# A fused chunk-attention and Mish feed-forward kernel: attention steps of the next tokens spread over two units, weight sums loaded one unit ahead, operands of x built in small steps

## The chip, the cores and the metric

The kernel runs on one core of one Trainium2 chip. The metric is device time in microseconds, median over the runs. Times are in us unless marked otherwise.

## The reference

Attention inside chunks of 64 tokens, then a feed-forward block with Mish (h tanh(softplus(h))), for 8 batches, 8 heads, 576 positions and head size 64, that is 4608 tokens of width 512 and a hidden width of 2048, all in float32.

```python
scores = scale * np.matmul(q_c, k_c.transpose(0, 1, 2, 4, 3))
scores = scores - np.max(scores, axis=-1, keepdims=True)
attn = np.exp(scores)
attn = attn / (np.sum(attn, axis=-1, keepdims=True) + 1e-09)
out = np.matmul(attn, v_c)
...
h = x @ w_in
sp = np.where(h > 20.0, h, np.log1p(np.exp(np.minimum(h, 20.0))))
g = h * np.tanh(sp)
return (g @ w_out).astype(np.float32)
```

The two weight matrices arrive as 64-bit floats and are turned into float32 by integer operations on the chip.

## The kernel before

**Precision.** The matmuls of the feed-forward block take operands in a reduced form of float32. Each operand is split into a high part (a cast on ACT or DVE) and a low part (a subtraction on DVE), and each product is three matmuls: low x high, high x low, high x high.

**Tokens.** A "pair" is two tiles of 128 tokens. The 18 pairs are worked off in five groups: two pairs first (512 tokens), then four quads of four pairs (1024 tokens each).

**First group.** `prologue` (line 469) does attention of the first two pairs. Then 16 `slot`s (line 543) run, one for each 128 columns of the hidden width (f = 0 to 15): `up` is the product with w_in, `mish` the activation on ACT, `g_split` makes gh and gl, and `down` queues 12 matmuls (4 token tiles x 3) of the product with w_out in the list `fill`, which `filled(n)` issues later. Beside this the slots load and convert the weights (`w_load` to `w_keep`; 32 blocks) and do attention of quad 1's four pairs, by the table `first_plan` (line 538).

**Quads.** The product with w_in uses a seven-product scheme (Strassen's in Winograd's form), with halves of the tokens and of the contraction: A11, A12, A22 are blocks of weights, S1 to S4 sums of blocks; B11, B21, B22 and T1 to T4 are the same of x. `s_load` (line 174) loads a converted block pair (cs) into the tile bld, and `s_build` (line 182) forms the four sums on DVE (line 195), a cast on ACT (196), the low part on DVE (197), and stores both to DRAM as sa. This happens once for each of the eight units, u = 0 to 7: two builds in the last two slots and six in quad 1's units, each load directly ahead of its build. `load_op` (line 630) loads one operand (w_A from ra or w_S from sa) six products ahead. `x_sums` (376) and `x_split` (367) make T1 to T4 and the parts of all seven operands of x, in two halves, out of `raw`, the result of attention.

**Unit** (line 696): seven products of six matmuls each go into the PSUM tiles x, y and v (two buffers). Between them stand 3 to 5 matmuls of `fill`, 24 in a unit. ACT and DVE turn the sums into four results: two (a1, a2) are split and queued for `down` at once, two (b1, b2) are kept in zb for the second half of the tokens. `phase_two` (line 750) does `down` for these, 16 f's of 12 matmuls. The results accumulate in PSUM banks o_(m, 0) and o_(m, 1); `store` (line 452) copies four tiles of them to the buffers ob (three) and then to DRAM. New banks can only begin where the old ones have been copied.

**Attention beside a quad.** The steps for a pair are a_scores (PE), a_max and a_sub (DVE), a_exp (ACT), a_inverse and a_norm (DVE), a_transpose (PE), a_copy (ACT), a_values (PE), a_raw (ACT). In the kernel before they follow the table `plan` (line 660) by ticks: three ticks in a unit and one for each step of phase_two. A pair's scores, exp, norm, transposes and values lie in consecutive ticks; the fourth pair's transposes and values fall into phase_two.

**Order.** The program runs under a manual schedule: each engine works its instructions in the order in which the code issues them, and waits at each for its operands and buffers. The loads, and the stores to DRAM, are on SP's queue, which is in order as well.

Of the kernel before, what the change touches and what calls it, by code (L numbers as in the profile page):

```python
# [14 lines left out]
ALU = mybir.AluOpType  # L15
# [8 lines left out]
def kernel(  # L24
# [149 lines left out]
    def s_load(u):  # L174
        if "t" not in bld:
            bld["t"] = zb_p.tile([P, 16 * 256], F32, name="bld", tag="z")
        t = bld["t"]
        nc.sync.dma_start(
            out=t[:, 0 : 2 * DM], in_=w_c[u].rearrange("p h c -> p (h c)")
        )  # L180

    def s_build(u):
# [6 lines left out]
        for out_, x, y, op in (  # L189
            (s1, a21, a22, ALU.add),  # L190
            (s2, s1, a11, ALU.subtract),
            (s3, a11, a21, ALU.subtract),
            (s4, a12, s2, ALU.subtract),
        ):
            nc.vector.tensor_tensor(out=out_, in0=x, in1=y, op=op)
        nc.scalar.copy(out=o[:, :, 0].bitcast(F32R), in_=s)
# [179 lines left out]
    def x_sums(m, half):  # L376
        for out_, x, y in (
            ("T1", "B12", "B11"),
            ("T3", "B22", "B12"),
            ("T2", "B22", "T1"),  # L380
            ("T4", "B21", "T2"),
        ):
            nc.vector.tensor_tensor(
                out=raw_half(m, half, out_),
                in0=raw_half(m, half, x),
                in1=raw_half(m, half, y),
                op=ALU.subtract,
            )
# [149 lines left out]
    first_plan = {}  # L538
    for i, k0 in enumerate((1, 4, 7, 10)):
        for n in range(-2, 4):  # L540
            first_plan.setdefault(k0 + n, {})[n] = first_pair(1) + i

    def slot(s):
        a = first_plan.get(s, {})
# [4 lines left out]
        if 3 in a:  # L549
            a_values(a[3])  # L550
        if s < NF - 1:
            filled()
        if 2 in a:
            a_norm(a[2])
            a_transpose(a[2])
        if 0 in a:
            a_scores(a[0])

# [3 lines left out]
        down(0, s, it[s])  # L562
# [3 lines left out]
        if 1 in a:  # L566
            a_max(a[1])
            a_sub(a[1])

        w("load", n + 5)  # L570
        w("keep", n)
        if 3 in a:
            a_raw(a[3])
        if 2 in a:
            a_copy(a[2])
# [8 lines left out]
        if 1 in a:  # L584
            a_exp(a[1])
            a_inverse(a[1])
        if -2 in a and a[-2] > 2:
            load_qk(a[-2], pool=(xo_p, "x"))
        if s == NF - 1:
            load_qk(first_pair(2))  # L590
        if 0 in a:
            load_v(a[0])
        if s == 9:
            x_split(1, 0, "B11", "B21")
        if s == 10:
# [12 lines left out]
        if s == 15:
            x_sums(1, 1)
            x_split(1, 1, "T2", "T1", "T3", "T4")  # L610
            s_load(1)
            s_build(1)
# [45 lines left out]
    TICKS = 3 * NU + NU  # L658
    plan = {}
    for i, k0 in enumerate((1, 8, 15, 22)):  # L660
        for n in range(0, 5):
            plan.setdefault(k0 + n, {})[n] = i
        plan.setdefault(max(0, k0 - 3), {})[-3] = i

    def pair_at(m, tick, n):
        i = plan.get(tick, {}).get(n)
        return None if i is None or m == QUADS else first_pair(m + 1) + i

    def on_tensor(m, tick):
        for n, step in ((3, a_transpose), (4, a_values), (0, a_scores)):  # L670
            j = pair_at(m, tick, n)
            if j is not None:
                step(j)

    def beside(m, tick):
        for n, steps_ in (
            (-3, () if tick == 0 else (load_qk,)),
            (0, (load_v, a_max, a_sub)),
            (1, (a_exp, a_inverse)),
            (2, (a_norm,)),  # L680
            (3, (a_copy,)),
            (4, (a_raw,)),
        ):
            j = pair_at(m, tick, n)
            for step in steps_ if j is not None else ():
                step(j)

    zb = {}
    BUILD = {0: 2, 2: 3, 4: 4, 6: 5, 8: 6, 10: 7}

    def build(m, tick):
        if m == 1 and tick in BUILD:
            s_load(BUILD[tick])
            s_build(BUILD[tick])

    def unit(m, u):
        tick = 3 * u
# [9 lines left out]
        on_tensor(m, tick)  # L707
# [5 lines left out]
        build(m, tick)  # L713
        beside(m, tick)

        product(m, u, 2, x, False)
        filled(3)
        nc.scalar.copy(out=b1, in_=x)  # L718
        on_tensor(m, tick + 1)
        y = ps_h.tile([P, TOK], F32, name=f"v_{m}_{u}", tag="h")  # L720
        product(m, u, 3, y, True)
        filled(5)
        g_split(a1, a1["z"], f"{m}_{2 * u}")
        build(m, tick + 1)
        beside(m, tick + 1)

        product(m, u, 4, x, False)
        filled(3)
        nc.scalar.copy(out=b2, in_=x)  # L729
        on_tensor(m, tick + 2)  # L730
        filled(2)
        product(m, u, 5, x, False)
        add(y, b2)
        a2["z"] = z_tile(f"z_{m}_{2 * u + 1}")
        mish(a2["z"], x)
        product(m, u, 6, y, False)
# [13 lines left out]
    def phase_two(m):  # L750
        after = m < QUADS
        p = first_pair(m)
        for i in range(NU):
# [3 lines left out]
            if i == 0:  # L757
                store(f"{m}a", (p, p + 2))
# [74 lines left out]
```

## Time and profile before

| | |
|---|---|
| median of 3 runs | 980.69 (980.15 to 981.61) |
| the profiled execution | 983.48, its span 981.6 |
| PE busy | 854.0 (87%), 5724 matmuls |
| DVE busy | 439.5 (45%) |
| ACT busy | 381.3 (39%) |
| DMA | 137.25 MB, 140 GB/s on average |
| mean granted TensorE clock | 0.942 |

The profile shows one execution. PE is the matmul engine, PEld its weight loads, DVE the vector engine, ACT the scalar engine, SPq the queue of DMA issues. A row names the line of the kernel, the engine, the operation, the tiles written and read (buffer numbers left out), and the shapes. Its times are busy time in total and the mean of one instruction in ns, then the idle time before it and what ended that. In rows by time the first number is the start and the second the duration; a matmul's duration includes its way through the array, so the distance between starts says what it costs. The granted clock is a share of full speed.

### The profile page before, as it was taken

The numbers are of one execution on the slowest core, as the hardware profiler recorded it, in microseconds if no ns is written. First come the engines' busy times: TensorE is split into PE (matmuls) and PEld (weight loads), VectorE is DVE, ScalarE is ACT, GpSimd is POOL, SyncE is SP. The second block draws the span as 40 slices with busy tenths as digits, with TensorE's granted clock in tenths as the row PEclk, the third lists the DMA queues.
The fourth block names the chain that finished last, engine by engine and source line by source line (L and its number), as shares of the span: only waits on it lengthen the run. The fifth ranks groups of instructions, "written<-read, shape, count | busy, mean of one in ns | idle before, by whom it ended". The sixth has DMA issues, their size and how long they took to land.

```text
span 981.6 us, 14157 instructions
## 1 busy us (share of the span) xinstructions
PE 854.0 (87%) x5724; PEld 690.9 (70%) x5724; DVE 439.5 (45%) x678; ACT 381.3 (39%) x584; POOL 0.7 (0%) x6
## 2 busy tenths in 40 slices
PE   4988855468599979989999799899997999999897
PEld 3866744356487858768778587687785877888685
DVE  6788983432524354433343444433424543223221
ACT  4878851322334233343342433433433433222221
POOL 0000000000000000000000000000000000000000
PEclk9899996778899989999999899999998999999999
DMA  6989816556554530256455301554453016444201
GB/s 247 334 291 302 284 67 228 179 175 201 171 184 131 170 85 21 68 127 185 149 140 165 93 22 44 151 182 146 135 152 95 1 43 161 119 130 120 52 1 43
DMA packets 68577, 137.25 MB, mean 140 GB/s; under 512 B 7072, under 2 KB 13216, under 8 KB 67488
## 3 DMA queue, kind: packets, MB, share of 16 engines
q1 hardware_dynamic: 68224, 135.82, 45.5%
q8 instruction: 46, 0.75, 0.3%
q10 hardware_dynamic: 288, 0.52, 0.1%
q14 instruction: 19, 0.16, 0.1%
HBM read 108.00 MB, written 28.31 MB: 139 GB/s over the span
## 4 chain that ended last, share of the span: by engine, by line
PE 65%; DVE 13%; ACT 7%; DMA 7%; issue 3%; SPq 1%; ACTq 0%; DVEq 0%
PE x L644 16%; PE v L644 8%; PE y L644 4%; DMA bld<-cs 3%; PE o_(4, 1)_0_7181 L435 2%; PE o_(4, 0)_0_6431 L435 2%; PE o_(4, 1)_2_7188 L435 2%; PE o_(1, 1)_0_2904 L435 2%; PE o_(3, 1)_0_6000 L435 2%; PE o_(2, 1)_0_4452 L435 2%; PE o_(4, 0)_2_6448 L435 2%; PE o_(1, 1)_2_2911 L435 2%; PE o_(2, 1)_2_4459 L435 2%; PE o_(3, 1)_2_6007 L435 2%; PE o_(3, 0)_0_4931 L435 2%
## 5 line engine op out<-in xcount | busy, mean ns | idle before, releaser
L644 PE MATMUL x<-x_T,w_S 128*128 128x512 f32 x384 | 102.7, 404 | 16.0 <-ACT zb L718 8.0
L656 DVE TENSOR_TENSOR zb<-v,zb 128x512 f32<-128x512 f32 x64 | 44.2, 690 | 126.4 <-PE v L644 94.8
L644 PEld LDWEIGHTS x<-x_T,w_S 128*128 128x128 f32 x384 | 74.3, 195 | 33.5 <-ACT zb L718 9.3
L422 DVE CAST gh<-z 128x512 fp32r<-128x512 f32 x72 | 30.5, 423 | 114.9 <-PE o_(4, 0)_2_6448 L435 28.4
L644 PE MATMUL x<-x_B,w_A 128*128 128x512 f32 x192 | 50.8, 401 | 12.9 <-DMA w_A<-ra 12.9
L294 PE MATMUL pt<-ident,p 128*128 128x128 f32 x144 | 24.3, 321 | 42.7 <-DVE p L285 35.6
L729 ACT COPY zb<-x 128x512 f32<-128x512 f32 x32 | 18.8, 587 | 108.6 <-PE x L644 108.6
L424 DVE TENSOR_TENSOR gl<-z,gh 128x512 fp32r<-128x512 f32 x80 | 55.4, 693 | 9.8 <-ACT gh L420 7.4
L294 PEld LDWEIGHTS pt<-ident,p 128*128 128x128 f32 x144 | 19.3, 165 | 49.2 <-issue 38.8
L415 ACT ACTIVATE z<-z 128x512 f32<-128x512 f32 x32 | 20.2, 632 | 86.6 <-DVE z L656 86.6
L644 PE MATMUL y<-x_B,w_A 128*128 128x512 f32 x192 | 53.6, 418 | 0.0
L656 DVE TENSOR_TENSOR z<-y,z 128x512 f32<-128x512 f32 x32 | 22.1, 690 | 69.7 <-PE y L644 69.7
L644 PEld LDWEIGHTS x<-x_B,w_A 128*128 128x128 f32 x192 | 36.4, 192 | 22.7 <-ACT x_T L371 13.3
L402 PE MATMUL h<-x_first,wi 128*128 128x512 f32 (+1 forms) x204 | 51.4, 407 | 0.7 <-ACT x_first L334 0.7
L644 PE MATMUL x<-x_T,w_A 128*128 128x512 f32 x192 | 50.8, 401 | 0.0
L644 PE MATMUL v<-x_T,w_S 128*128 128x512 f32 x192 | 50.5, 398 | 0.1
L415 ACT ACTIVATE zb<-zb 128x512 f32<-128x512 f32 x64 | 39.6, 627 | 25.1 <-DVE zb L656 25.1
L644 PE MATMUL v<-x_B,w_S 128*128 128x512 f32 x192 | 49.0, 391 | 0.0
L402 PEld LDWEIGHTS h<-x_first,wi 128*128 128x128 f32 x204 | 39.4, 208 | 8.6 <-ACT x_first L334 0.9
L415 ACT ACTIVATE z<-x 128x512 f32<-128x512 f32 x32 | 19.1, 597 | 67.5 <-PE x L644 67.4
L644 PEld LDWEIGHTS y<-x_B,w_A 128*128 128x128 f32 x192 | 38.4, 204 | 8.8
L644 PEld LDWEIGHTS x<-x_T,w_A 128*128 128x128 f32 x192 | 37.6, 196 | 8.4
(197 smaller groups left out, 1794.7 us busy)
## 6 DMA issues: line engine op xcount, KB each, us to landing
w_S<-sa SPq DMA_DIRECT2D x128, 256.0 KB, 3.2
w_A<-ra SPq DMA_DIRECT2D x96, 256.0 KB, 2.8
wst<-in_w_in SPq DMA_DIRECT2D x16, 512.0 KB, 5.8
wst<-in_w_out SPq DMA_DIRECT2D x16, 512.0 KB, 5.7
q<-in_q SPq DMA_DIRECT2D x16, 512.0 KB, 4.0
k<-in_k SPq DMA_DIRECT2D x16, 512.0 KB, 5.6
v<-in_v SPq DMA_DIRECT2D x16, 512.0 KB, 4.5
sa<-bld SPq DMA_DIRECT2D x8, 1024.0 KB, 4.9
```

Source lines behind the costliest of these rows:

```text
L294: nc.tensor.transpose(out=d["pt", ts.start][:, t - ts.start, g], in_=d["p"][:, t, g].rearrange("p c k -> p (c k)"), identity=ident,)
L402: nc.tensor.matmul(h[:, cols], lhsT=wi[i][:, w_, kt], rhs=x[:, x_, kt, cols], start=(n == 0), stop=(n == 3 * NK - 1),)
L415: nc.scalar.activation(out=out_, in_=in_, func=AF.Mish)
L422: nc.vector.tensor_copy(out=d["gh"], in_=z)
L424: nc.vector.tensor_tensor(out=d["gl"], in0=z, in1=d["gh"].bitcast(F32), op=ALU.subtract)
L435: nc.tensor.matmul(acc[t], lhsT=g[:, t * P : (t + 1) * P], rhs=w_[:, f], start=(f == 0 and n == 0), stop=(f == NF - 1 and n == 2),)
L644: nc.tensor.matmul(o, lhsT=t[:, w_, kt], rhs=x[x_][:, kt], start=(start and i == 0), stop=(i == 5), skip_group_check=not start,)
L656: nc.vector.tensor_tensor(out=z, in0=o, in1=z, op=ALU.add)
L729: nc.scalar.copy(out=b2, in_=x)
```

## The change

The computation and the number of instructions of each kind on PE and DVE stay the same. What changes is where they stand.

1. *Builds.* `s_build(u)` itself issues the load of the next block pair after its four sums. `s_load(0)` goes to slot 13, `s_build(0)` to slot 14 ahead of the x steps, `s_build(1)` to slot 15 behind them. Builds 2 to 7 are spread over units 0 to 3 of quad 1, at two places in a unit. Two of the first six operand loads go ahead of `s_load(0)`.
2. *Attention in the slots* follows two tables by half slots, `on_pe` and `beside_pe`, and takes seven half slots for a pair. `filled()` and `down` move behind the first half's work on ACT and DVE.
3. *Attention in the units.* Each pair takes two units: scores after product 0 of the even unit, max and sub after product 1, exp after product 2, inverse after product 3, norm after product 4, transposes and copy at its end; values and raw in the odd unit, and the loads of the next q and k behind them. The last pair's raw waits for phase_two.
4. *Unit.* `filled` is dealt out as 3, 5, 4, 4, 5 and the rest. Copy, add and mish of b2 follow product 4. In unit 0 the whole fill is issued after product 4 and the store of the previous group follows there, instead of after the unit.
5. *phase_two* goes by single f's: 12 matmuls, the split of one f, then two of the 23 small x steps. The store comes at f = 1.

```diff
@@ s_load, s_build
     def s_load(u):
+        if u >= NU:
+            return
...
             nc.vector.tensor_tensor(out=out_, in0=x, in1=y, op=op)
+        s_load(u + 1)
         nc.scalar.copy(out=o[:, :, 0].bitcast(F32R), in_=s)
@@ x
+    X_STEPS = [
+        ("B11",),
+        ("B21",),
+        ("B22",),
+        ("T1", "B12", "B11"),
+        ("T3", "B22", "B12"),
+        ("T2", "B22", "T1"),
+        ("T4", "B21", "T2"),
+        ("T2",),
+        ("T3",),
+        ("T1",),
+        ("T4",),
+    ]
+
+    def x_step(m, half, n):
+        step = X_STEPS[n]
+        if len(step) == 1:
+            x_split(m, half, *step)
+        else:
+            x_sum(m, half, *step)
@@ slots
-    for i, k0 in enumerate((1, 4, 7, 10)):
...
+    for i, h0 in enumerate((1, 8, 15, 22)):
+        j = first_pair(1) + i
+        for n, step in ((0, a_scores), (5, a_transpose), (6, a_values)):
+            on_pe.setdefault(h0 + n, []).append((step, j))
+        for n, steps_ in (
+            (0, (load_v,)),
+            (1, (a_max, a_sub)),
+            (2, (a_exp,)),
+            (3, (a_inverse,)),
+            (4, (a_norm,)),
+            (5, (a_copy,)),
+            (6, (a_raw,)),
+        ):
...
+    for s, steps_ in ((9, (0, 1)), (10, (2, 3)), (11, (4, 5, 6)), (12, (7, 8)), (13, (9,)), (14, (10,))):
...
+        if s == NF - 3:
+            load_op()
+            load_op()
+            s_load(0)
+        if s == NF - 2:
+            s_build(0)
+            for i in range(LOOK - 2):
+                load_op()
+        run(beside_pe, 2 * s + 1)
         if s == NF - 1:
+            s_build(1)
             load_qk(first_pair(2))
@@ unit
+        begins, ends = m < QUADS and u % 2 == 0, m < QUADS and u % 2 == 1
...
-        on_tensor(m, tick)
+        if begins:
+            a_scores(j)
+            load_v(j)
...
+        if begins:
+            a_max(j)
+            a_sub(j)
+        if ends:
+            a_values(j)
+            if u < NU - 1:
+                a_raw(j)
+                load_qk(j + 1)
+        if m == 1 and (u, 0) in BUILDS:
+            s_build(BUILDS[u, 0])
...
-        filled(3)
+        filled(5 if u else None)
         nc.scalar.copy(out=b2, in_=x)
-        on_tensor(m, tick + 2)
-        filled(2)
+        add(y, b2)
+        mish(b2, b2)
+        if u == 0:
+            if m == 1:
+                store("0", (0, 1))
+            else:
+                p = first_pair(m - 1)
+                store(f"{m - 1}b", (p + 1, p + 3))
+        if begins:
+            a_norm(j)
...
+        if begins:
+            a_transpose(j)
+            a_copy(j)
@@ phase_two
-        for i in range(NU):
...
+        for f in range(NF):
+            filled(12)
+            if f == 1:
                 store(f"{m}a", (p, p + 2))
+            d = {}
+            g_split(d, z_of(f), f"{m}b_{f}", True)
+            down((m, 1), f, d)
+            for _ in range(2):
+                if todo:
+                    todo.pop(0)()
```

The first place is SP's queue between the last slots and quad 1's first unit. cs_1 is the input of build 1, sa_0 and sa_1 are the stored sums, w1_0_... the first unit's operands, q_6 and k_6 the inputs of the scores in that unit. Before:

```order
L635 DMA w1_0_A22_1583<-ra_0_100 128x512
L209 DMA q_6_1589<-in_q 128x2x512
L209 DMA k_6_1590<-in_k 128x2x512
L178 DMA bld_1564<-cs_1_117 128x1024
L198 DMA sa_1_109<-bld_1564 128x2048
L635 DMA w1_0_S4_1622<-sa_0_108 128x512
```

Now:

```order
L179 DMA bld_1484<-cs_1_117 128x1024
L200 DMA sa_0_108<-bld_1484 128x2048
L645 DMA w1_0_S2_1568<-sa_0_108 128x512
L645 DMA w1_0_S1_1570<-sa_0_108 128x512
L645 DMA w1_0_S3_1572<-sa_0_108 128x512
L645 DMA w1_0_A22_1574<-ra_0_100 128x512
L179 DMA bld_1484<-cs_2_118 128x1024
L200 DMA sa_1_109<-bld_1484 128x2048
L211 DMA q_6_1610<-in_q 128x2x512
L211 DMA k_6_1611<-in_k 128x2x512
```

The loads of q_6 and k_6 stood ahead of build 1's load; now they stand behind its store, and each cs load is issued ahead of the store of the build before.

The second place is DVE in the second phase of quad 2. gl_2b_0 and so on are the low parts for f = 0, 1, ..., x3_... the low parts of quad 3's operands, raw_10 and raw_11 the in-place sums, ob the store's copies. Before:

```order
L424 TENSOR_TENSOR gl_2b_3_4484<-zb_2_0_3209,gh_2b_3_4482 128x512
L383 TENSOR_TENSOR raw_10_3527<-raw_11_3859,raw_10_3527 128x4x128
L383 TENSOR_TENSOR raw_11_3859<-raw_11_3859 128x4x128
L383 TENSOR_TENSOR raw_11_3859<-raw_11_3859,raw_10_3527 128x4x128
L383 TENSOR_TENSOR raw_10_3527<-raw_10_3527,raw_11_3859 128x4x128
L372 TENSOR_TENSOR x3_T2_1_4494<-raw_11_3859,x3_T2_0_4492 128x4x2x64
L372 TENSOR_TENSOR x3_T1_1_4498<-raw_10_3527,x3_T1_0_4496 128x4x2x64
L372 TENSOR_TENSOR x3_T3_1_4502<-raw_11_3859,x3_T3_0_4500 128x4x2x64
L372 TENSOR_TENSOR x3_T4_1_4506<-raw_10_3527,x3_T4_0_4504 128x4x2x64
L424 TENSOR_TENSOR gl_2b_4_4567<-zb_2_0_3209,gh_2b_4_4565 128x512
```

Now:

```order
L441 TENSOR_TENSOR gl_2b_0_4441<-zb_2_0_3209,gh_2b_0_4439 128x512
L374 TENSOR_TENSOR x3_B11_1_4445<-raw_10_3450,x3_B11_0_4443 128x4x2x64
L374 TENSOR_TENSOR x3_B21_1_4449<-raw_10_3450,x3_B21_0_4447 128x4x2x64
L473 COPY ob_2a_1_4467<-o_(2, 0)_0_3395 128x512
L473 COPY ob_2a_3_4475<-o_(2, 0)_2_3412 128x512
L441 TENSOR_TENSOR gl_2b_1_4481<-zb_2_0_3209,gh_2b_1_4479 128x512
L374 TENSOR_TENSOR x3_B22_1_4485<-raw_11_3751,x3_B22_0_4483 128x4x2x64
L379 TENSOR_TENSOR raw_10_3450<-raw_11_3751,raw_10_3450 128x4x128
L441 TENSOR_TENSOR gl_2b_2_4504<-zb_2_0_3209,gh_2b_2_4502 128x512
```

Eight x steps stood between gl of f = 3 and gl of f = 4; now two stand between neighbouring f's, and the store's two DVE copies between f = 0 and f = 1.

The third place is DVE in unit 0 of quad 2. m_10, p_10 and r_10 are attention of pair 10, ob_1b the store of the group before, zb and z the unit's own adds. Before:

```order
L278 TENSOR_REDUCE r_10_0_3353<-p_10_3307 128x8x2
L279 TENSOR_SCALAR r_10_0_3353<-r_10_0_3353 128x16
L280 RECIPROCAL r_10_0_3353<-r_10_0_3353 128x16
L456 COPY ob_1b_1_3361<-o_(1, 1)_0_2904 128x512
L456 COPY ob_1b_3_3369<-o_(1, 1)_2_2911 128x512
L656 TENSOR_TENSOR z_2_2_3373<-y_2_1_3388,z_2_2_3373 128x512
L285 TENSOR_TENSOR p_10_3307<-p_10_3307,r_10_0_3353 128x2x8x64
```

Now:

```order
L280 TENSOR_REDUCE r_10_0_3310<-p_10_3277 128x8x2
L281 TENSOR_SCALAR r_10_0_3310<-r_10_0_3310 128x16
L282 RECIPROCAL r_10_0_3310<-r_10_0_3310 128x16
L666 TENSOR_TENSOR zb_2_0_3209<-v_2_0_3293,zb_2_0_3209 128x512
L473 COPY ob_1b_1_3337<-o_(1, 1)_0_2940 128x512
L473 COPY ob_1b_3_3345<-o_(1, 1)_2_2947 128x512
L287 TENSOR_TENSOR p_10_3277<-p_10_3277,r_10_0_3310 128x2x8x64
L666 TENSOR_TENSOR zb_2_0_3209<-v_2_0_3293,zb_2_0_3209 128x512
L439 CAST gh_2_1_3370<-z_2_1_3358 128x512
```

The store's copies stood behind the unit's last add and ahead of the next unit's first; now they stand inside the unit, between the two adds of zb, and a_norm (the row that writes p_10) and the second add are behind them.

More of the change, by code (lines that the diff above doesn't have):

```diff
@@ L374, in x_split, with x_sum @@
             )
[L376 to L388, printed above, removed]
+    def x_sum(m, half, out_, x, y):
+        nc.vector.tensor_tensor(
+            out=raw_half(m, half, out_),
+            in0=raw_half(m, half, x),
+            in1=raw_half(m, half, y),
+            op=ALU.subtract,
+        )
+    X_STEPS = [
[17 more added lines that the diff above has]
+            x_sum(m, half, *step)
     it = {}
@@ L536, in prologue, with run @@
             w("keep", n)
[L538 to L541 removed]
+    on_pe, beside_pe = {}, {}
+    for i, h0 in enumerate((1, 8, 15, 22)):
[11 more added lines that the diff above has]
+        ):
+            beside_pe.setdefault(h0 + n, []).extend((step, j) for step in steps_)
+        if i:
+            beside_pe.setdefault(h0 - 6, []).append((lambda j: load_qk(j, pool=(xo_p, "x")), j))
+    for s, steps_ in ((9, (0, 1)), (10, (2, 3)), (11, (4, 5, 6)), (12, (7, 8)), (13, (9,)), (14, (10,))):
+        beside_pe.setdefault(2 * s + 1, []).extend(
+            (lambda n: x_step(1, 0, n), n) for n in steps_
+        )
+    beside_pe.setdefault(29, []).extend((lambda n: x_step(1, 1, n), n) for n in range(5))
+    beside_pe.setdefault(31, []).extend((lambda n: x_step(1, 1, n), n) for n in range(5, 11))
+    def run(plan_, key):
+        for step, arg in plan_.get(key, ()):
+            step(arg)
     def slot(s):
[L544 removed]
         n = 2 * s + 3
@@ L548, in slot @@
             up(s + 1, last="w")
[L549 to L557, printed above, removed]
+        run(on_pe, 2 * s)
         w("load", n + 4)
@@ L656, in add @@
         nc.vector.tensor_tensor(out=z, in0=o, in1=z, op=ALU.add)
[L658 to L686, printed above, removed]
-    zb = {}
[L689 to L694, printed above, removed]
+    zb = {}
+    BUILDS = {(0, 1): 2, (1, 0): 3, (1, 1): 4, (2, 0): 5, (2, 1): 6, (3, 0): 7}
     def unit(m, u):
-        tick = 3 * u
+        j = first_pair(m + 1) + u // 2
+        begins, ends = m < QUADS and u % 2 == 0, m < QUADS and u % 2 == 1
         if u % 4 == 0:
@@ L741, in unit @@
         g_split(a2, a2["z"], f"{m}_{2 * u + 1}")
-        build(m, tick + 2)
-        beside(m, tick + 2)
+        if begins:
+            a_transpose(j)
+            a_copy(j)
         down((m, 0), 2 * u, a1)
```

94 lines of the change are left out of this document (20 added, 74 removed).

## Prediction

> **What bounds the kernel now.** I read the span first, then cut it at the kernel's own stages in the view by windows (columns: window, its length, busy time of PE, PEld, DVE, ACT and POOL with instruction counts, granted TensorE clock, DMA share, GB/s).
>
> ```profile
> span 981.6 us, 14157 instructions
> ```
>
> ```profile
> 38.00:133.60 95.60, 83.00 (x838) 66.63 (x837) 81.91 (x123) 74.57 (x115) 0.00 (x0) 0.98 0.82 277
> 133.60:165.70 32.10, 13.53 (x47) 9.95 (x45) 19.85 (x35) 11.70 (x20) 0.00 (x0) 0.78 0.44 147
> 165.70:344.30 178.60, 143.13 (x981) 113.92 (x982) 68.67 (x107) 54.51 (x77) 0.00 (x0) 0.89 0.56 175
> 344.30:403.40 59.10, 50.20 (x265) 40.66 (x265) 29.04 (x46) 22.38 (x36) 0.00 (x0) 0.91 0.16 42
> 403.40:542.20 138.80, 134.28 (x1002) 108.88 (x1001) 52.39 (x77) 51.24 (x74) 0.00 (x0) 0.99 0.53 150
> 542.20:601.20 59.00, 50.09 (x265) 40.58 (x264) 29.10 (x46) 22.38 (x36) 0.00 (x0) 0.91 0.17 43
> 601.20:740.20 139.00, 134.48 (x1002) 109.03 (x1001) 52.42 (x77) 51.25 (x74) 0.00 (x0) 0.99 0.52 149
> 740.20:799.20 59.00, 50.09 (x266) 40.55 (x265) 29.07 (x46) 22.38 (x36) 0.00 (x0) 0.91 0.10 24
> 799.20:920.20 121.00, 120.39 (x530) 99.14 (x529) 35.31 (x57) 35.27 (x59) 0.00 (x0) 1.00 0.43 118
> 920.20:981.60 61.40, 50.85 (x216) 41.29 (x215) 14.81 (x23) 12.74 (x21) 0.00 (x0) 0.94 0.15 35
> ```
>
> The rows are: the slots; the passage from the last slots to the third product of the first unit; the rest of quad 1's units; its second phase; then units and second phase of quads 2, 3 and 4. Quad 4, without attention, keeps PE busy 120.39 of 121.00. Quad 1's units need 178.6 for work that takes quads 2 and 3 139, with a clock of 0.89 against 0.99. The second phases of quads 1 to 3 stand still for 9 of 59. So I looked at who waits for whom in quad 1's units (total, times, longest), and on PE at the price of a matmul and of attention.
>
> ```profile
> DVE bld L195 <- DMA bld<-cs: 24.9, 6, 7.6
> ...
> PE o_(1, 0)_0_1803 L435 <- DVE ob L456: 10.9, 1, 10.9
> ```
>
> ```profile
> 601.21 1.52 PE L644 MATMUL x<-x_B,w_A 128*128 128x512 f32 x6
> 602.57 0.39 PE L435 MATMUL o_(2, 1)_0_4452<-wo_h,gl_2b 128*128 128x512 f32 x1
> ...
> 607.88 1.16 PE L226 MATMUL s<-k,q 64*64 64x64 f32 x64
> 608.97 1.66 PE L644 MATMUL v<-x_T,w_S 128*128 128x512 f32 x6
> 610.47 0.39 PE L435 MATMUL o_(2, 1)_2_4459<-wo_h,gh_2b 128*128 128x512 f32 x1
> ```
>
> ```profile
> 177.81 2.93 PE L644 MATMUL x<-x_T,w_S 128*128 128x512 f32 x6 [4.53 <-ACT zb L718]
> ```
>
> Six matmuls issue in 602.57 - 601.21 = 1.36, so one takes 0.227. Scores of a pair cost 610.47 - 607.88 - 1.36 = 1.23; I take 1.2 for transposes and values too. After a wait of 4.53 the same six last 2.93 instead of 1.52: a long wait costs some 1.7 more, as a slow clock. The whole DVE stands behind each cs load, and ACT and PE behind the DVE.
>
> **The change, stage by stage.** The durations of the moved steps:
>
> ```profile
> L372 DVE TENSOR_TENSOR x_T<-raw,x_T 128x512 fp32r<-128x512 f32 x32 | 20.1, 686 | 0.9 <-ACT x_T L371 0.9
> ...
> L285 DVE TENSOR_TENSOR p<-p,r 128x1024 f32<-128x1024 f32 x16 | 19.5, 1219 | 0.1
> ...
> L195 DVE TENSOR_TENSOR bld<-bld 128x256 f32<-128x256 f32 x32 | 12.2, 421 | 34.3 <-DMA bld<-cs 34.0
> ...
> L197 DVE TENSOR_TENSOR bld<-bld 128x1024 fp32r<-128x1024 f32 x8 | 9.8, 1225 | 9.2 <-ACT bld L196 9.2
> ...
> L729 ACT COPY zb<-x 128x512 f32<-128x512 f32 x32 | 18.8, 587 | 108.6 <-PE x L644 108.6
> ...
> L415 ACT ACTIVATE zb<-zb 128x512 f32<-128x512 f32 x64 | 39.6, 627 | 25.1 <-DVE zb L656 25.1
> ```
>
> *Second phases, quads 1 to 3.* Sixteen groups of 12 matmuls issue in 192 x 0.227 = 43.5. Per f the DVE now has one gl and two x steps, each 128x512 like the L372 row, 3 x 0.69 = 2.07, against 12 x 0.227 = 2.72 on PE, so the operands hide; before, eight x steps in a row (5.5) stood ahead of the next gl. What is late next is the store: o_(m, 1) reuses the banks that it reads, and its fourth copy needs the buffer of the first, whose transfer must land.
>
> ```profile
> 618.39 1.28 ACT L273 ACT_TABLE_LOAD   x1
> 619.68 1.06 ACT L273 ACTIVATE p<-p 128x1024 f32<-128x1024 f32 x1
> 620.64 0.57 ACT L458 COPY ob_2b<-o_(2, 1)_0_4452 128x512 f32<-128x512 f32 x1
> ...
> 624.22 0.69 DVE L456 COPY ob_2b<-o_(2, 1)_2_4459 128x512 f32<-128x512 f32 x1 [1.19 <-DMA out<-ob_2b]
> ```
>
> The fourth copy starts 624.22 - 621.21 = 3.0 after the first ends. With two x splits ahead of the store on ACT and DVE, I reckon PE waits 0.9 for the first bank pair and 1.3 for the second. So 43.5 + 2.3 = 45.8 instead of 59.0, or -13.2 each, -39.6 in all. Two transposes-and-values steps (2.4) are part of this and reappear in the units.
>
> *Units of quads 2 and 3.* 528 matmuls give 119.7, four pairs with three steps each 14.4 (before: ten steps, 12): 134.1. From the start of an even unit product 4 ends at 5 x 1.36 + 16 x 0.227 + 1.2 = 11.7 and product 6, with the rest of the fill, at 16.3. Copy b2 ends 0.2 + 0.59 later, at 12.5; add(y, b2) at 13.2; a_norm at 14.5, 1.8 ahead of the transposes; a_copy is done 3 ahead of the values. load_qk holds SP until the values are issued, 2.5 at most, and six products' loads are ahead. Unit 0 is the exception. There the store stands in the DVE's queue ahead of a_norm, and behind a_norm PE waits with the transposes. On ACT copy b2, table load, mish(b2) and the store's first copy take 0.59 + 1.28 + 0.63 + 0.57 from 11.9, so that copy ends at 15.0; the fourth runs 18.0 to 18.7, a_norm to 19.9, while product 6 is issued by 16.3. PE waits 3.7 and pays 1.7 for the slow clock. 134.1 + 5.4 = 139.5 against 138.9: +1 for both quads. Before, 138.9 - 119.7 - 12 leaves 7 for waits, so little changes.
>
> Against this change stands a rule of the Trainium skill, page "ScalarE: Activation LUTs", section "What ACT_TABLE_LOAD costs": a switch of tables costs 1283 ns and a drain of about 1380 ns more. The rows above disagree: the load begins at 618.39 and exp at 619.68, with no drain between. By the page two switches would delay unit 0's store by 2.8, and the sum would be 8 higher over three quads.
>
> *Quad 1's units after its third product.* Of 134.1 there remain 128.4 (less two products, eight matmuls and scores). Loads of cs are issued half a unit ahead, at least 7, and waited 24.9 / 6 = 4.2 each, 7.6 at most, so the DVE finds them there. A build still holds the DVE for 4 x 0.421 + 1.225 = 2.9 plus a cast on ACT. I count 1.0 + 0.4 + 0.5 + 0.6 of waits in unit 2, where two builds meet max and sub; 1 after unit 0's build; and unit 0's 5.4. That is 137.3 instead of 178.6: -41.3. If a build cannot hide, it costs up to its 4, so 6 x 4 = 24 more is the upper end.
>
> *The passage.* Here the change takes something back. load_qk for quad 1's first pair is now queued on SP behind the store of sa_1, which waits for the DVE's last step of s_build(1), and PE needs it before product 1 instead of after product 2. (The first products' own loads are ahead of it on SP, and S2's lands some 20 before use.)
>
> ```profile
> 133.99 0.42 DVE L422 CAST gh<-z 128x512 fp32r<-128x512 f32 x1
> ```
>
> ```profile
> k<-in_k SPq DMA_DIRECT2D x16, 512.0 KB, 5.6
> ```
>
> From this cast (slot 13's) the DVE of the changed kernel has 22 steps of 0.69, two of 0.42, one of 1.22 and two builds of 2.9: 23.1, and with waits for casts on ACT and the first cs load about 28. It reaches the cast some 2 earlier (a_norm and one split stand behind it instead of ahead), so it ends at 160. q and k are issued by 161, land 5.6 to 7.6 later, say at 167.5; scores, product 1 and five matmuls at the slow clock take 6. The third product starts at 173.5 instead of 165.7: +7.8. Inside the slots attention is spread evenly, but the DVE's work (81.91 of 95.6) stays; I take -1.8, with ends of -4.6 (PE's own 16-slot work closed up) and +4 (ps copies later on ACT). Together +6.
>
> *Quad 4 and the end.* One wait of 0.65 in its units, -0.6; its second phase has the store's wait but no x steps, -2.1 as an estimate from the 2.3 above and the 4.2 by which its 53.2 before the end exceed 216 x 0.227 = 49.
>
> **Sum.** +6 - 41.3 - 39.6 + 1 - 0.6 - 2.1 = -76.6. The profiled execution took 983.48, so 906.9; the median of the runs shown is 980.69, 2.8 less, so I predict 904.1 for the median.
>
> **Rivals.**
> 1. *The passage is short and the store does not cool the clock* (faster still). Slots -4.6 instead of -1.8, k after 5.6 (-0.9), no slow clock after unit 0's wait (3 x 1.7): 895. For it speaks that PE idles 12.6 in the slots; against it the DVE's load there. Chance 0.2.
> 2. *The small steps are late* (faster, but less). Each x step on the DVE waits for a cast on ACT, which waits for a sum on the DVE; if that chain adds one 0.69 per f for the twelve f's that carry steps, it is 8.3 per quad, 25 in all: 929. The busy shares of ACT (22.38 of 59) and DVE (29.04) speak against it. Chance 0.2.
> 3. *The early load does not come early.* s_load(u+1) stands on SP behind the DVE's sums, then behind products' loads; if it lands late as before, 24.9 of waits stay and about 10 of slow clock: 939. Then the change does not do what it says. Chance 0.06.
>
> ```profile
> PE pt L294 <- DVE p L285: 35.6, 14, 7.7
> ```
>
> 4. *Slower than before.* The transposes end each even unit and need a_norm, which is queued behind add(y, b2), which needs the copy after product 4, which follows exp. This place occurs 12 times. If a_norm came more than 76.6 / 12 = 6.4 late each time (slow clock included), the gain would be gone; a wait of 7.7, the longest in the row above, plus 1.7 gives 113 and a time of 1017.
>
> Against it is the slack of 1.8 counted above, so it takes 8 of delay in each unit. Chance 0.03.
>
> **How the numbers follow.** My forecast has 0.5, and 0.01 is left for gains and losses that cancel. The range 888 to 928 takes in the forecast with its open terms (passage -6 to +5, builds up to +10) and rival 1, and reaches to rival 2's edge; rivals 3 and 4 are left out. Runs of this kernel differ by 0.15%, so about 0.2% can be told from no change. Faster: 0.5 + 0.2 + 0.2 + 0.06 = 0.96; within: 0.01; slower: 0.03.
>
> **What would show it.** Right: in the changed profile no DVE wait for bld<-cs over 1 in quad 1's units; second phases of 46 with PE waiting only for ob copies; scores of the first pair waiting over 10 for k; a wait for a_norm once per quad, in unit 0. Wrong: units of quads 2 and 3 above 145 (rival 4, by waits of pt for p), second phases above 52 (rival 2, by waits for gl), quad 1's units above 155 (rival 3). A passage that ends before 165 would show that the load of q and k was not late.

## The result, and the profile after

| | before | after |
|---|---|---|
| median | 980.48 (980.15 to 981.61, 4 runs) | 902.53 (900.59 to 904.89, 4 runs) |
| profiled execution, its span | 983.48, 981.6 | 900.59, 898.8 |

The ratio is 0.9204, 95% interval 0.9181 to 0.9228: 78 faster, 1.6 from the forecast of 904.1. The view by windows of the changed kernel, cut at the same stages (slots, passage to the third product, the rest of quad 1's units, its second phase, and so on; columns as in the prediction):

```profile
38.00:126.30 88.30, 79.38 (x701) 64.43 (x700) 76.64 (x117) 72.89 (x112) 0.00 (x0) 0.96 0.83 297
126.30:169.50 43.20, 18.51 (x185) 14.37 (x184) 25.22 (x43) 14.01 (x24) 0.00 (x0) 0.72 0.51 171
169.50:305.30 135.80, 131.06 (x989) 105.92 (x989) 69.36 (x109) 60.20 (x81) 0.00 (x0) 0.99 0.69 213
305.30:351.00 45.70, 44.13 (x193) 35.88 (x192) 26.36 (x42) 19.14 (x33) 0.00 (x0) 1.00 0.19 54
351.00:488.60 137.60, 134.04 (x1073) 109.91 (x1072) 55.62 (x81) 56.47 (x77) 0.00 (x0) 1.00 0.54 151
488.60:534.40 45.80, 44.22 (x194) 35.96 (x193) 26.34 (x42) 19.13 (x33) 0.00 (x0) 1.00 0.20 54
534.40:674.70 140.30, 136.75 (x1073) 112.08 (x1072) 55.59 (x81) 56.49 (x77) 0.00 (x0) 0.98 0.53 148
674.70:720.40 45.70, 44.07 (x193) 35.85 (x193) 26.38 (x42) 19.13 (x33) 0.00 (x0) 1.00 0.13 32
720.40:840.00 119.60, 119.32 (x527) 98.51 (x526) 34.59 (x56) 34.87 (x58) 0.00 (x0) 1.00 0.44 119
840.00:898.80 58.80, 50.44 (x220) 40.78 (x219) 15.55 (x23) 12.86 (x21) 0.00 (x0) 0.97 0.16 36
```

The clock of quad 1's units went from 0.89 to 0.99 and their length from 178.6 to 135.8 with the same products. Each second phase lost 13.3. The passage is still the emptiest stretch: PE is busy 18.51 of 43.20, at a clock of 0.72.

| stage | before | forecast | after |
|---|---|---|---|
| to the third product | 165.7 | +6 | 169.5 (+3.9) |
| quad 1's units after it | 178.6 | -41.3 | 135.8 (-42.8) |
| second phases, quads 1 to 3 | 59.1, 59.0, 59.0 | -39.6 in all | 45.7, 45.8, 45.7 (-39.9) |
| units, quads 2 and 3 | 138.8, 139.0 | +1 in all | 137.6, 140.3 (+0.1) |
| quad 4, units | 121.0 | -0.6 | 119.6 (-1.4) |
| quad 4, the rest | 61.4 | -2.1 | 58.8 (-2.6) |

Who waits for whom, in the view of PE's waits (total, times, longest):

```profile
PE s L228 <- DMA k<-in_k: 22.6, 2, 17.9
PE pt L296 <- DVE p L287: 18.9, 5, 5.9
...
PE o_(3, 1)_2_6043 L452 <- DVE ob_3a L473: 1.1, 1, 1.1
...
PE o_(3, 1)_0_6036 L452 <- DVE ob_3a L473: 0.5, 1, 0.5
```

The longest wait is the new one for k. Of the waits for a_norm (p), 18.9 in all, three are the first units', 10.7 together. In the second phases only the store's copies are waited for, 0.5 and 1.1. In the profile's list of groups the DVE's sums of weights, which had waited 34.0 for cs, now wait 0.6:

```profile
L196 DVE TENSOR_TENSOR bld<-bld 128x256 f32<-128x256 f32 x32 | 12.1, 420 | 0.9 <-DMA bld<-cs 0.6
```

PE in the passage and at the first unit's transposes, in the timeline (start, time, instruction, the wait ahead of it):

```profile
164.31 1.98 PE L228 MATMUL s<-k,q 64*64 64x64 f32 x64 [17.86 <-DMA k<-in_k]
...
169.55 1.52 PE L654 MATMUL x<-x_T,w_S 128*128 128x512 f32 x6
...
183.71 1.06 PE L296 MATMUL pt<-ident,p 128*128 128x128 f32 x8 [3.57 <-DVE p L287]
184.53 2.64 PE L654 MATMUL x<-x_B,w_A 128*128 128x512 f32 x6
...
371.03 1.06 PE L296 MATMUL pt<-ident,p 128*128 128x128 f32 x8 [3.56 <-DVE p L287]
371.85 1.64 PE L654 MATMUL x<-x_B,w_A 128*128 128x512 f32 x6
...
554.30 1.94 PE L296 MATMUL pt<-ident,p 128*128 128x128 f32 x8 [3.55 <-DVE p L287]
```

### The profile page after: what moved, and what is told of

Its sections match the earlier page's. It is cut to its first block, busy times and chain, and to the rows that moved or that the text cites. A ratio compares the mean times of both kernels' runs of the same rounds, so it can differ in the third digit from the quotient of the medians.

```text
span 898.8 us, 14182 instructions
## 1 busy us (share of the span) xinstructions
PE 827.2 (92%) x5724; PEld 675.1 (75%) x5724; DVE 438.7 (49%) x678; ACT 387.9 (43%) x584; POOL 0.7 (0%) x6
## 4 chain that ended last, share of the span: by engine, by line
PE 77%; DVE 9%; ACT 6%; DMA 5%; issue 3%; SPq 0%; DVEq 0%; ACTq 0%
PE x L654 18%; PE v L654 9%; PE y L654 5%; PE o_(4, 0)_0_6431 L452 2%; PE o_(3, 0)_0_4943 L452 2%; PE o_(1, 1)_2_2947 L452 2%; PE o_(3, 1)_2_6043 L452 2%; PE o_(2, 1)_2_4495 L452 2%; PE o_(4, 1)_2_7188 L452 2%; PE o_(3, 0)_2_4960 L452 2%; PE o_(2, 0)_2_3412 L452 2%; PE o_(4, 1)_0_7181 L452 2%; PE o_(2, 0)_0_3395 L452 2%; PE o_(4, 0)_2_6448 L452 2%; PE av L228 2%
## 5 line engine op out<-in xcount | busy, mean ns | idle before, releaser
L654 PE MATMUL x<-x_T,w_S 128*128 128x512 f32 x384 | 99.2, 394 | 0.6 <-ACT zb L704 0.6
L654 PEld LDWEIGHTS x<-x_T,w_S 128*128 128x128 f32 x384 | 71.1, 188 | 16.1 <-ACT zb L704 1.1
L441 DVE TENSOR_TENSOR gl<-z,gh 128x512 fp32r<-128x512 f32 x80 | 55.3, 692 | 13.7 <-ACT gh L437 11.2
L296 PE MATMUL pt<-ident,p 128*128 128x128 f32 x144 | 23.7, 315 | 32.7 <-DVE p L287 18.9
L654 PE MATMUL x<-x_B,w_A 128*128 128x512 f32 x192 | 52.6, 410 | 0.9 <-ACT x_B L373 0.7
L654 PE MATMUL y<-x_B,w_A 128*128 128x512 f32 x192 | 51.6, 405 | 0.6 <-DVE zb L666 0.6
L654 PE MATMUL x<-x_T,w_A 128*128 128x512 f32 x192 | 48.9, 390 | 0.1
L654 PE MATMUL v<-x_T,w_S 128*128 128x512 f32 x192 | 48.7, 389 | 0.0
L654 PEld LDWEIGHTS y<-x_B,w_A 128*128 128x128 f32 x192 | 35.8, 193 | 9.6 <-DVE zb L666 1.8
L228 PE MATMUL s<-k,q 64*64 64x64 f32 x1088 | 21.7, 232 | 22.7 <-DMA k<-in_k 22.6
L654 PEld LDWEIGHTS v<-x_B,w_S 128*128 128x128 f32 x192 | 36.0, 188 | 8.0 <-DVE zb L666 0.6
```

The source lines that it names most:

```text
L228: nc.tensor.matmul(o[h * CHUNK : (h + 1) * CHUNK, c, t - ts.start, g], lhsT=l[rows, t, 2 * g + h], rhs=r[rows, t, 2 * g + h], start=True, ...
L296: nc.tensor.transpose(out=d["pt", ts.start][:, t - ts.start, g], in_=d["p"][:, t, g].rearrange("p c k -> p (c k)"), identity=ident,)
L441: nc.vector.tensor_tensor(out=d["gl"], in0=z, in1=d["gh"].bitcast(F32), op=ALU.subtract)
L654: nc.tensor.matmul(o, lhsT=t[:, w_, kt], rhs=x[x_][:, kt], start=(start and i == 0), stop=(i == 5), skip_group_check=not start,)
```

## Experiments

The theory was the prediction's, with one amendment from the two traces: that most of what the second phases lost was the fourth pair's attention, and little of it the small x steps. Each ratio is against the kernel before on the same chip.

| run | median | ratio, 95% interval |
|---|---|---|
| e3_load_late | 942.78 | 0.960 (0.957 to 0.963) |
| e5_before_early | 949.09 | 0.966 (0.964 to 0.968) |
| e4_x_lumped | 916.02 | 0.933 (0.930 to 0.935) |
| e6_last_pair_late | 922.46 | 0.938 (0.936 to 0.941) |
| e1_qk_early | 892.32 | 0.909 (0.906 to 0.912) |
| e2_norm_first | 893.66 | 0.909 (0.907 to 0.911) |
| e7_qk_norm_b1 | 880.18 | 0.895 (0.893 to 0.897) |
| e8_all_pt_late | 879.94 | 0.895 (0.893 to 0.897) |
| e9_builds_later | 875.14 | 0.890 (0.887 to 0.893) |
| e10_same | 900.00 | 0.916 (0.912 to 0.920) |

The changed kernel stands at 902.53 and, run once more (e10_same), at 900.00, so differences from it are read as from 900.0 to 902.5.

**The early load undone alone.**

```diff
 def s_build(u):
+    s_load(u)
...
-    s_load(u + 1)
...
-            s_load(0)
```

> The changed kernel with the early loads undone alone: each cs load is queued directly ahead of its own build, as in the kernel before; the builds' places, attention's steps and x's small steps stay. Theory (the early load is what removed quad 1's waits): DVE waits 4 to 5 for cs in each of the six builds again, 25 in all, with slow matmuls behind some of them; quad 1's units go from 135.8 to 165 to 180 and the time rises by 30 to 45, to about 940. Rival (the new places of the builds and the spread of attention hide the waits, and the loads need not be early): quad 1's units stay under 146, the time rises by 10 or less.

It rose by 40 to 43. The DVE's timeline at the first two of the six builds in quad 1's units:

```profile
191.44 1.55 DVE L197 TENSOR_TENSOR bld<-bld 128x256 f32<-128x256 f32 x4 [5.61 <-DMA bld<-cs]
...
207.98 1.55 DVE L197 TENSOR_TENSOR bld<-bld 128x256 f32<-128x256 f32 x4 [8.22 <-DMA bld<-cs]
```

And PE behind them:

```profile
196.03 2.93 PE L653 MATMUL y<-x_B,w_A 128*128 128x512 f32 x6 [6.92 <-DVE zb L665]
...
211.19 2.81 PE L653 MATMUL x<-x_T,w_S 128*128 128x512 f32 x6 [4.23 <-ACT zb L703]
```

Six DVE waits of 4.0 to 8.2 come back, and each becomes a PE wait of 3.6 to 6.9 (27.9 in all) on a copy or add queued behind the build, with slow matmuls after it. From the third product on, quad 1's units take 174.3 instead of 135.8. The rival, that the new places alone hide the loads, is out.

**The early load alone, in the kernel before.**

```diff
             nc.vector.tensor_tensor(out=out_, in0=x, in1=y, op=op)
+        s_load(u + 1)
...
-            s_load(1)
             s_build(1)
...
-            s_load(BUILD[tick])
```

> The kernel before with the early loads alone: each cs load is queued inside the build ahead of it, the builds' places, attention and x's steps stay as they were. Theory (the early load is what removed quad 1's waits): the 24.9 of DVE waits for cs go and the long PE waits behind them with their slow matmuls; quad 1's units fall from 178.6 to about 150 and the time by 25 to 40, to 940 to 955. Rival (the loads alone do little, since builds and attention steps still meet in the same gaps between products): the time falls by less than 15.

It fell by 33.5, as the theory has it. The one DVE wait for cs that is left (seven with 34.0 in the kernel before), and the third product in PE's timeline:

```profile
DVE bld L197 <- DMA bld<-cs: 3.6, 1, 3.6
```

```profile
158.53 1.52 PE L646 MATMUL x<-x_T,w_S 128*128 128x512 f32 x6
```

It starts 7.2 earlier than in the kernel before, and the units from there on end at 310.9, after 152.4 instead of 178.6. Between that and 135.8 lie 16.6 more. By PE's waits the largest part of these is the first group's store. Its copies are still queued on the DVE behind a build and a step of attention, and PE waits for them in unit 1, where the kernel before waited 10.9:

```profile
PE o_(1, 0)_0_1804 L438 <- DVE ob L459: 7.2, 1, 7.2
```

The product behind that wait takes 2.76 instead of 1.52. The run above, with the late loads in the new order, has no such wait, so it is the new order that removes it: the store now stands inside unit 0, ahead of the build. What the store's place, the builds' places and the spread attention are worth each, no run separates. So the one line of the load is over 40% of the whole gain, and part of it lies in the passage.

**x's steps in lumps again.**

```diff
-            for _ in range(2):
+            for _ in range({1: 3, 3: 8, 5: 1, 9: 3, 11: 8}.get(f, 0)):
```

> The changed kernel with the x steps of the second phases done in lumps of 3 and 8 at the places where the kernel before had them (behind the operands of f = 1, 3, 9 and 11); the attention of the fourth pair stays in the units, the fills stay one f at a time. Theory, formed from the two traces (of the 13.2 that each second phase lost, most was the fourth pair's transposes and values with their waits, and only about 2 the lumps): each second phase grows by 1 to 4.4, the time by 3 to 13, to about 909. Rival, which the prediction's text leaned on (the eight steps in a row ahead of the next gl are what cost): each second phase grows by 8 or more, the time by 24 or more, to over 926.

It rose by 13.5 to 16, somewhat above the theory's upper end and far from the rival's 24. The view of PE's waits has in each second phase a row like this one of quad 1:

```profile
PE o_(1, 1)_0_2939 L452 <- DVE gl_1b L441: 3.7, 2, 1.8
```

Each row of eight x steps delays the next gl by 1.85, twice per quad. By windows the second phases take 50.2, 51.8 and 51.9 instead of 45.7, the last two at a clock of 0.97. So the lumps cost 4.5 to 6.2 here. In the kernel before they cost less, since PE waited for gl only once in a second phase, behind the second row of eight:

```profile
396.06 0.50 PE L435 MATMUL o_(1, 1)_0_2904<-wo_h,gl_1b 128*128 128x512 f32 x1 [1.85 <-DVE gl_1b L424]
```

The 24 matmuls from there to the next unit take 7.2 instead of 5.4, because eight of them run at the slow clock. Wait and slow clock together are 3.6 of the 13.3.

**The fourth pair's attention back in the second phase.**

```diff
-        begins, ends = m < QUADS and u % 2 == 0, m < QUADS and u % 2 == 1
+        begins, ends = m < QUADS and u % 2 == 0 and u < 6, m < QUADS and u % 2 == 1 and u < 7
+        late = m < QUADS and u == 7
...
+        if late:
+            a_scores(j)
...
+            if after and f == 2:
+                a_transpose(j)
+            if after and f == 4:
+                a_values(j)
             filled(12)
...
+            if after and f == 1:
+                a_norm(j)
```

> The changed kernel with the attention of each quad's fourth pair put back where the kernel before had it: scores after the third product of the last unit, max and sub behind them, norm behind the operands of f = 1 in the second phase, transposes ahead of f = 2's matmuls, values ahead of f = 4's. x's small steps and single fills stay. Theory (most of the 13.2 that each second phase lost was this pair): PE waits 4 to 6 for a_norm and pays 1 to 2 of slow clock, so each second phase grows by 7 to 10 (2.4 of it taken from the units), the time by 15 to 24, to 918 to 927. Rival (the waits came from the DVE's lumps of x steps, which are gone): PE finds a_norm done, each second phase grows by its own 2.4 alone, and the time changes by less than 5.

It rose by 20 to 22. PE's timeline in the first second phase:

```profile
314.79 1.94 PE L296 MATMUL pt<-ident,p 128*128 128x128 f32 x8 [5.27 <-DVE p L287]
...
324.85 1.16 PE L228 MATMUL av<-ps,v 64*64 64x64 f32 x64 [1.62 <-ACT ps L306]
```

The kernel before has the same two waits in each second phase, the first of them

```profile
355.16 1.94 PE L294 MATMUL pt<-ident,p 128*128 128x128 f32 x8 [5.44 <-DVE p L285]
```

Here they stand without any lump of x steps: a_norm is queued behind the store's copies and the operands of two f's, and PE has nothing between it and the transposes. Second phases take 55.2, 55.8 and 54.9, that is 9.2 to 10 more, of which about 2.4 leaves the units. With the 3.6 that the lumps cost in the kernel before, that is 12.8 to 13.6 against the measured 13.3, so hardly anything is left for a third cause. The amendment stands.

**q and k of the first unit loaded earlier.**

```diff
         if s == NF - 2:
+            load_qk(first_pair(2))
             s_build(0)
...
             s_build(1)
-            load_qk(first_pair(2))
```

> The changed kernel with one call moved: the loads of q and k for quad 1's first unit are queued ahead of the first build of sums instead of behind the second build. In the changed kernel PE's first scores wait 17.86 for k. Theory (the queue place behind the second build's store is the whole cause of that wait): k lands before 150, the scores no longer wait for it, the third product starts at about 156 instead of 169.55, and the time falls by 12 to 14, to about 889. Rival (the second build's own chain, whose sums and x parts the third product needs, is as late as k): the scores come early but the third product still waits, for T2 or S2, until 165 or later, and the time falls by less than 5.

It fell by 8 to 10, less than the theory and more than the rival. On PE:

```profile
147.36 1.16 PE L228 MATMUL s<-k,q 64*64 64x64 f32 x64
...
156.44 2.93 PE L654 MATMUL x<-x_T,w_S 128*128 128x512 f32 x6 [5.20 <-ACT z L682]
```

The wait for k is gone, so its cause was the place on SP's queue, and the third product starts 13.1 earlier, where the theory had it. But PE still waits 5.20 there, now for the copy of the first product on ACT, which stands behind the second build's cast; the matmuls after it are slow (six in 2.93 instead of 1.52), and by windows the units after the third product take 139.6 instead of 135.8. Those 3.8 are the shortfall.

**a_norm ahead of the store.**

```diff
         mish(b2, b2)
+        if begins:
+            a_norm(j)
         if u == 0:
...
-        if begins:
-            a_norm(j)
         product(m, u, 5, x, False)
```

> The changed kernel with a_norm of each quad's first unit ahead of the store's four copies instead of behind them. In the changed kernel PE waits 3.56 for that a_norm in each of three quads, and in two of the three quads the clock was low after it. Theory: the wait goes (3 x 3.56 = 10.7) and with it the slow matmuls behind it (1 to 2 each), nothing else is late, so the time falls by 11 to 15, to about 889. Rival (the store has to finish before the next unit's results anyway, so the wait only moves): PE waits instead in the next unit for the adds queued behind the store's copies, and the time falls by less than 4.

It fell by 6 to 9, between the theory and the rival. In quads 2 and 3 no wait for a_norm is left, and their units take 133.9 and 134.3 instead of 137.6 and 140.3: the theory. In quad 1 the rival holds: its units take 136.0, like the changed kernel's 135.8, because PE now waits in unit 1 for an add of unit 0, which is queued on the DVE behind the store's copies and a build:

```profile
188.60 1.71 PE L654 MATMUL y<-x_B,w_A 128*128 128x512 f32 x6 [3.85 <-DVE zb L666]
```

**Three moves together, and two further ones.** The first kernel has both edits above and the second build moved into the first unit; the second delays the fourth pair's transposes in the slots; the third has the first's moves with the builds half a unit later.

```diff
-            s_build(1)
...
-    BUILDS = {(0, 1): 2, (1, 0): 3, (1, 1): 4, (2, 0): 5, (2, 1): 6, (3, 0): 7}
+    BUILDS = {(0, 0): 1, (0, 1): 2, (1, 0): 3, (1, 1): 4, (2, 0): 5, (2, 1): 6, (3, 0): 7}
```

> The changed kernel with three moves: q and k of quad 1's first unit loaded ahead of the first build, a_norm ahead of the store in each first unit, and the second build moved out of the last slot into the first unit (behind its second product's operands). The first alone gave 892.3, the second alone 893.7 on a chip where the kernel before had 982.9. Theory (the waits are separate, and the 5.2 that PE still waited for a copy queued behind the second build's cast goes too): the gains add up, 10.2 + 8.9 + 5, less 2 for the build in the unit, so about 880. Rival (the DVE in the first unit is full once it has two builds and a store, so the time only moves into that unit): quad 1's units grow by 6 or more, and the time stays above 888.

The median is 880.18, as the theory has it. The third product starts at 153.51, 16.0 earlier than in the changed kernel. But quad 1's units take 141.1 instead of 135.8, 5.3 more where the theory took 2, so the rival has part of the truth: PE waits 6.0 in unit 1 for an add queued on the DVE (row below).

```diff
-            on_pe.setdefault(h0 + n, []).append((step, j))
+            on_pe.setdefault(h0 + n + (i == 3 and n > 0), []).append((step, j))
...
-            beside_pe.setdefault(h0 + n, []).extend((step, j) for step in steps_)
+            beside_pe.setdefault(h0 + n + (i == 3 and n > 4), []).extend((step, j) for step in steps_)
```

> The kernel with the three moves, and in the slots the transposes, values and copies of the fourth pair half a slot later each, behind the next product with w_in. In the changed kernel PE waited 5.93 for a_norm there. Theory (PE has 2.7 of that product's matmuls ready and they fill the wait): PE waits 3 instead of 5.9, the time falls by 2 to 5 against the three moves alone. Rival (the DVE is the bound of the last slots, it works without a gap from 112 to 134): PE waits as long at a later place, the time changes by less than 1.5.

The wait at the transposes falls from 5.94 to 3.22, and the median is the same (879.94 against 880.18). In time the rival holds: 2.7 less of waiting of PE there is worth nothing that can be told from none. Its reason, that the DVE bounds the last slots, is not shown: in this profile the third product starts at 151.76, which is 1.75 earlier, after a wait of 2.80 for an operand of the first build (S2).

```diff
+    BUILDS = {(0, 0): 1, (1, 0): 2, (1, 1): 3, (2, 0): 4, (2, 1): 5, (3, 0): 6, (3, 1): 7}
```

> The three moves of the run before, with the seven builds of quad 1's units half a unit later from the second one on, so that the first unit holds one build (behind its second product) instead of two and the last stands in the second half of the fourth unit. With two builds PE waited 6.0 in unit 1 for an add that was queued on the DVE behind the store's copies and the second of them, and then ran six matmuls in 2.93. Theory (the second build is 4.0 of that wait): the wait falls to about 2, the slow matmuls go, and the time falls by 5 to 6 against the 880.2 of the three moves, to about 875. Rival (the tile of the sums is the buffer that the fifth unit's results need, and the last build's store now frees it too late): PE waits 3 or more in the fifth unit, and the time stays above 878.

The median is 875.14, the best of all: 0.890 of the kernel before, and 25 to 27 below the changed kernel. The place in unit 1, with two builds in the first unit (the three moves):

```profile
175.33 2.93 PE L652 MATMUL y<-x_B,w_A 128*128 128x512 f32 x6 [6.00 <-DVE zb L664]
```

and with one:

```profile
170.40 2.09 PE L652 MATMUL y<-x_B,w_A 128*128 128x512 f32 x6 [2.46 <-DVE zb L664]
```

PE has no wait over 1.8 in the rest of quad 1's units, so the last build's store is not too late.

**The same kernel again.** No edit.

> The changed kernel unaltered, as a base on this chip and for the clock: in its first profile the same wait of 3.55 to 3.57 ahead of the first unit's transposes was followed by transposes in 1.06 in quads 1 and 2 and in 1.94 in quad 3. Theory (the clock's step down does not depend on the place, it falls where the clock's own beat meets the gap): the three waits come out at 3.5 to 3.6 again, but which of them the slow transposes follow, or whether any, changes. Rival (something of each quad's own decides it): quad 3 alone is slow again. The time is 900 to 906 by both.

The time is 900.00. The three waits are 3.57, 3.55 and 3.56, and the transposes after them take the same times as in the first profile: 1.06, 1.06 and 1.94. So the theory's forecast that the pattern changes from run to run fails. The rival fails as well, by the other kernels: with x in lumps the same wait of 3.54 in quad 3 is followed by 1.06 and six matmuls at full speed, and in the kernel with q and k early quad 1's is followed by 1.94. What decides it is where the clock's own beat cuts the wait, as the last section works out; the theory had that part right. In these two profiles the beat falls at nearly the same place in each wait, and why it does stays open.

## Why the prediction was right, step by step

**Quad 1's units** (-41.3, measured -42.8). Right in size, and in its reason as far as the loads go: cs is found loaded when the DVE comes to it (0.6 of waits left in the whole kernel), and both experiments on this line agree. But the text put all that the stage lost on the loads. The 10.9 for the first group's store, which its own view of waits shows, was no term of its own, and the run with the early load alone keeps 7.2 of it. The size came out because the new stage was added up from its matmuls. The four waits that I counted in unit 2 and the one after unit 0's build (3.5) became three of PE's, 0.65, 0.15 and 0.31, with 1.1 in all; the longest is

```profile
213.74 1.65 PE L654 MATMUL x<-x_T,w_S 128*128 128x512 f32 x6 [0.65 <-ACT zb L704]
```

So a build hides almost entirely.

**Second phases** (-39.6, measured -39.9). The size is right; the store's waits are 0.5 and 1.1 against 0.9 and 1.3. The reason was only half told. The text let the row of eight x steps stand for what the kernel before lost; by the experiments and the row at 396.06 they are about 3.6 of 13.3, and 9.2 to 10 are the fourth pair's attention, with its 5.4 wait for a_norm and the slow clock behind it. The prediction mentioned only that pair's own 2.4. The sum came out because I built the new second phase from its matmuls up (43.5 plus the store) and did not subtract causes from the old one.

**The passage** (+6, measured +3.9). The mechanism, q and k queued behind the second build's store, is shown by the run with the early load. In size: the DVE's cast of slot 13, in its timeline

```profile
128.95 0.42 DVE L439 CAST gh<-z 128x512 fp32r<-128x512 f32 x1
```

came 1.2 earlier than I had it (133.99 - 2 - 1.8 = 130.2). The window up to that cast, in the kernel before

```profile
38.00:133.99 95.99, 83.39 (x840) 66.94 (x839) 82.30 (x124) 74.96 (x116) 0.00 (x0) 0.98 0.81 276
```

and after:

```profile
38.00:128.95 90.95, 80.45 (x705) 65.00 (x703) 79.22 (x121) 75.39 (x116) 0.00 (x0) 0.96 0.82 293
```

The DVE's idle time fell from 95.99 - 82.30 = 13.7 to 90.95 - 79.22 = 11.7, that is by 2.0 where I took 1.8; the work moved behind the cast is 3.1 and not 2. From there, on SP's queue,

```profile
156.19 0.32 SPq L200 DMA_DIRECT2D sa<-bld  x1
...
157.03 0.95 SPq L211 DMA_DIRECT2D k<-in_k  x1
```

the store's issue comes 27.2 after the cast (28 forecast), k lands 7.3 after its issue (5.6 to 7.6), and the third product follows 5.2 after the scores begin (6). The term was 2.1 too large: 1.2 from the cast, 0.8 from the chain and 0.8 from the scores and products, less 0.8 for k, which I had landing 6.5 after its issue.

**Units of quads 2 and 3** (+1, measured +0.1). The wait in unit 0 was forecast at 3.7 and is 3.56. The 1.7 for the slow clock was taken for each; it fell on quad 3, not on quad 2, and goes with the 2.7 between the two. Which quad it falls on was luck for the forecast: by the last section the place of the clock's beat decides it. The floor of 134.1 is confirmed by the run without the wait, at 133.9 and 134.3. ACT in unit 0 of quad 2 reads

```profile
359.05 1.28 ACT L275 ACT_TABLE_LOAD   x1
360.34 1.06 ACT L275 ACTIVATE p<-p 128x1024 f32<-128x1024 f32 x1
...
363.58 1.28 ACT L432 ACT_TABLE_LOAD   x1
364.88 0.63 ACT L432 ACTIVATE zb<-zb 128x512 f32<-128x512 f32 x1
365.42 0.57 ACT L475 COPY ob_1b<-o_(1, 1)_0_2940 128x512 f32<-128x512 f32 x1
```

Both times the function starts as the table load ends, and the store's copy directly behind it. By the rule of the Trainium skill (page "ScalarE: Activation LUTs", section "What ACT_TABLE_LOAD costs") the two drains would have made the wait 3.7 + 2.8 = 6.5; it is 3.56, so the row decided rightly.

**Rivals.** The small steps are not late: no wait for gl is in the second phases. The early load comes early. a_norm holds up PE in the units only in unit 0, by 3.6 and not 8. Of the faster rival, only the missing slow clock in quad 2 came true.

**The sum.** Each term came out from 0.3 to 2.1 on the faster side, 6 in all: the profiled execution took 900.6 against 906.9. That the median came within 1.6 of the forecast is partly luck: 4.7 of the 6.3 were given back because the profiled execution lay 2.8 above the median before and 1.9 below it after.

## What to carry to other kernels

Where a load is queued directly ahead of the work that needs it, on an engine that others wait behind, look for the waits that it causes: each such load here cost a wait of 4.0 to 8.2 on that engine, one of 3.6 to 6.9 on PE behind it, and slow matmuls after that (the run with the early load undone). Issuing it one step earlier was the largest single part here, and the runs show no price for it. When loads are moved on an in-order queue, look at what now stands behind a store that waits for the end of a long chain: q and k there gave back 8 to 10 of the gain. To forecast a stage, build it up from its matmuls and the waits that remain, since what the old stage lost can have another cause than the one that the change names.

## What the runs showed of the hardware

The clock's step down after a wait is neither sure at 3.5 nor absent below it. After waits of 3.54 to 3.58 ahead of the same transposes, the changed kernel's matmuls were slow from the first one (554.30), slow from 0.8 later (184.53, six in 2.64 behind transposes in 1.06), or not at all (371.85, six in 1.64). In the kernel before, two waits of 2.90 and 2.60 were followed by slow matmuls, and one of 3.27 was not:

```profile
54.67 1.06 PE L294 MATMUL pt<-ident,p 128*128 128x128 f32 x8 [3.27 <-DVE p L285]
...
237.41 2.93 PE L644 MATMUL x<-x_T,w_S 128*128 128x512 f32 x6 [2.90 <-ACT zb L718]
...
253.49 2.35 PE L644 MATMUL x<-x_T,w_S 128*128 128x512 f32 x6 [2.60 <-ACT z L706]
```

Even the wait of 1.85 in the kernel before, in the row at 396.06 above, was followed by eight slow matmuls, 0.43 apart instead of 0.23, from 397.56 on.

The granted clock of the traces says what decides. It changes only on a beat of 3.41: in all twelve traces every stretch of half clock that ends inside the trace is one to six times 3.41 long, and all of a run lie on one beat. Cut the run at this beat, and the idle time of PE within one stretch (by the matmul ends that the profile models) goes with the clock of the next. The view by windows for PE alone (window, length, busy time and instructions, granted clock, DMA share, GB/s) has, at the waits of quads 2 and 3 in the changed kernel,

```profile
365.75:369.16 3.41, 1.72 (x8) 1.00 0.53 122
369.16:372.57 3.41, 1.54 (x11) 1.00 0.85 199
372.57:375.99 3.42, 3.42 (x16) 1.00 0.75 199
550.07:553.48 3.41, 0.68 (x4) 1.00 0.82 187
553.48:556.90 3.42, 2.60 (x11) 0.50 0.83 173
```

and at the wait of 1.85 in the kernel before

```profile
394.13:397.54 3.41, 1.56 (x7) 1.00 0.00 0
397.54:400.95 3.41, 3.41 (x9) 0.50 0.00 0
```

In quad 2 the beat cuts the wait into 1.69 and 1.87 of idle time, and the clock stays up. In quad 3 it leaves 2.73 in one stretch, and the next one is at half clock. Over the full-speed stretches of the twelve traces, none of the 2812 with at most 1.81 idle was followed by half clock, all of the 99 with at least 1.94 were, and 8 of the 16 between. So by these traces a wait of PE of up to 1.8 does not lower the clock by itself, one above 3.9 always does, since the beat cannot cut it into two parts below 1.94, and in between the place of the beat decides. A slow stretch that PE fills loses half of its 3.41, which is the 1.7 that the prediction charged for a long wait.

The Trainium skill, page "TensorE: Matmul & The Clock Gate", Part 1, has the clock fall after an idle window of about 3.4, watched by a window that runs freely. The length of the window agrees with the beat in these traces. That the whole window has to be idle does not: 1.94 of 3.41 were enough.
